# Weight conversion: its addition and subtraction from GpSimd to VectorE, and the norm multiplications of batch 1 from VectorE to GpSimd

## The chip, the cores and the metric

The kernel runs on one core of one Trainium2 chip. The metric is the time of one execution on the device in microseconds (us), the median of several runs. The engines are called as the profile calls them: PE is TensorE (PEld its weight loads), DVE is VectorE, ACT is ScalarE, POOL is GpSimd, SP is SyncE, which here issues the DMAs (SPq is its queue).

## What is computed

The reference takes q, k and v of shape 8 x 12 x 448 x 64 and two weight matrices that the host holds in float64. Eight batches go through attention with a norm, a Fourier mix and a two-layer network:

```python
q_n, k_n = rmsnorm(q, g_q), rmsnorm(k, g_k)       # over the 64 of a head
scores = matmul(q_n, k_n.T) / sqrt(64)
attn = softmax(scores)
x = matmul(attn, v)                               # to (8, 448, 768)
mixed = real(fft(fft(x, axis=1), axis=2))
u = x + mixed
un = (u - mean(u)) / sqrt(var(u) + 1e-6)
out = u + maximum(un @ w_ch1, 0) @ w_ch2          # 768 -> 3072 -> 768
```

## The kernel before

The work is written per batch in two streams. `aux(b)` is the side stream: attention of the six head pairs, then the Fourier mix and the token norm, which leave the input of the network. `ffn(b, unT)` is the main stream: 24 blocks `up(m)` (18 matmuls each, L997) and 36 blocks `down(g, d)` (12 matmuls each, L1018). Batch 0's `aux` stands first; from step 112 on some steps of `aux(1)` go in between. Then `merge` lays `ffn(b)` and `aux(b + 1)` beside each other by a ratio of costs, for batch after batch. The instructions are written in this order; a planner that simulates a timeline when the kernel is built puts each engine's instructions in their final order, and an engine then works through its own queue strictly in that order. An instruction whose input is late holds up all that stand behind it on its engine.

Attention of a pair begins with `norm_pair(b, p)`, numbered `nth = 6 b + p`: ACT squares the raw q and k, DVE sums the squares and scales the sums (tile `ss`), POOL raises them to the power -1/2, and two multiplications of 112 x 512 elements each write the normed q and k (tile `qkn`). The two run on POOL for `nth` 2 to 8, and on DVE for `nth` 0, 1 and from 9 on (L276). Behind them PE transposes `qkn` (tile `qk`). In `softmax_pair` DVE takes the minimum of a score tile in PSUM (`mn`), ACT makes the exponentials (`P`) and their sums (`sm`); batch 0 then has DVE build diagonal matrices (`dg`), with which PE scales, and later batches scale `P` in place, partly on DVE. `fold` is a row of DVE additions and subtractions in SBUF (`eo`, `sd`).

The weights arrive as float64 and are converted to float32 once, in the first batch, and split into a rounded part and a rest; each converted piece goes to DRAM (L807) and is read back from there for later batches. There are 60 pieces: 24 of 128 x 768 elements for the first layer, 36 of 128 x 512 for the second. `convert` (L746) makes one piece of the two 32-bit halves `high` and `low` of each number. In order: ACT takes the absolute value of `high` into `mag` (L756) and scales `low` (L758); DVE clamps, shifts and merges in the sign (L763, L767, L771); POOL adds `low` to `mag` (L775); ACT copies the sum into the rounded part of `w` (L776); POOL subtracts that from the sum, which gives the rest (L777). The helper `behind` only adds ordering edges. The raw halves lie in four `dbl` buffers and the result of the first steps in three `mag` buffers, so that a later piece waits until L777 has freed a `mag` buffer, and its load (L753) until L775 has freed a `dbl` one. Some pieces (`w1e`, `w2e` in names) are converted beside `aux(0)`, the rest when `W1.load` and `W2.load` first reach them. All conversions lie between 20 and 468 us of the trace. The matmuls of `up` and `down` wait for their piece; its DRAM copy and all other loads stand in the one SP queue.

Of the kernel before, what the change touches and what calls it, by code (L numbers as in the profile page):

```python
# [16 lines left out]
ALU = mybir.AluOpType  # L17
# [7 lines left out]
NPAIR = H // 2  # L25
# [66 lines left out]
def spectral_block(ctx, tc, q, k, v, g_q, g_k, w1, w2, d1, d2, out, nb=B):  # L92
    nc = tc.nc
# [27 lines left out]
    V, A, G = Recorded(nc.vector), Recorded(nc.scalar), Recorded(nc.gpsimd)  # L121
    starting = [True]

    def order(ins, before, kind, reason):
        tc.add_manual_dep(
            ins.ins, before.ins.name, mybir.DependencyInfo(kind, reason),
            reason="issue order",
        )
# [3 lines left out]
    def behind(ins):  # L132

        others = given.get(ins.ins.engine, [])
        if ins.ins.engine in gate:
            order(
                ins, gate[ins.ins.engine],
                mybir.DependencyClass.NoSync, mybir.DependencyReason.DATA,
            )
        if starting[0] and len(others) > LAG:  # L140
            order(
                ins, others[-1 - LAG],
                mybir.DependencyClass.NoSync, mybir.DependencyReason.DATA,
            )
# [117 lines left out]
    def norm_pair(b, p):  # L262
        raw = loaded.pop((b, p))
        qk = sb.tile([C, 2, NC, 2, D], F32, tag="qk", name=f"qkn{b}_{p}", bufs=1)
        sq = qk.rearrange("t i c h d -> t (i c h) d")
        flat = raw.rearrange("t i h c d -> t (i h c) d")
        nth = b * NPAIR + p
        A.activation(sq, flat, AF.Square)
        ss = sb.tile([C, 16], F32, tag="ss", name=f"ss{b}_{p}")
        V.tensor_reduce(ss, sq, axis=AX.X, op=ALU.add)  # L270
        V.tensor_scalar(
            out=ss, in0=ss, scalar1=1.0 / D, scalar2=EPS, op0=ALU.mult, op1=ALU.add
        )
        G.tensor_tensor(out=ss, in0=ss, in1=nhalf[:C], op=ALU.pow)
        for i in range(2):
            (G if 2 <= nth < NPAIR * 3 // 2 else V).tensor_tensor(  # L276
                out=qk[:, i].rearrange("t c h d -> t h c d"),
                in0=raw[:, i],
                in1=ss[:, 8 * i : 8 * i + 8]
                .rearrange("t (h c) -> t h c", h=2)[:, :, :, None]  # L280
                .broadcast_to([C, 2, NC, D]),
                op=ALU.mult,
            )
        if plain(b, p):
            return qk, None
        vt = values_of[b, p]
        vhl = sb.tile([128, 4, 4, D], F32R, tag="vhl", name=f"vhl{b}_{p}", bufs=1)
        A.copy(vhl[:, :, ::3], vt)
        (G if b < EARLY else V).tensor_tensor(
            out=vhl[:, :, 1:3], in0=vt, in1=vhl[:, :, ::3], op=ALU.subtract  # L290
        )
        return qk, vhl
# [5 lines left out]
    def plain(b, p):  # L298


        return b * NPAIR + p in PLAIN_PAIRS
# [4 lines left out]
    def transpose_pair(b, p):  # L306
# [3 lines left out]
        load_pair(b, p)  # L310
        load_pair(*next_pair(b, p))
        qk, vhl = norm_pair(b, p)
        yield 0

# [431 lines left out]
    def convert(src, bits, part, name):  # L746

        _, c, f = src.shape  # L750
        raw = sb.tile([128, 1536], U32, tag="dbl", name=f"dbl{name}", bufs=4)
        raw = raw[:, : c * f].rearrange("r (c f w) -> r c f w", c=c, w=2)
        nc.sync.dma_start(raw.rearrange("r c f w -> r c (f w)"), src)  # L753
        low, high = raw[:, :, :, 0], raw[:, :, :, 1]
        value = bits.bitcast(F32)
        first = nc.scalar.activation(value, high.bitcast(F32), AF.Abs)  # L756
        behind(first)
        second = nc.scalar.activation(low, low, AF.Copy, scale=2.0**-29)  # L758
        behind(second)
        order(  # L760
            second, first, mybir.DependencyClass.NoSync, mybir.DependencyReason.DATA
        )
        behind(nc.vector.tensor_scalar(  # L763
            out=value, in0=value, scalar1=MIN_HIGH, scalar2=MAX_HIGH,
            op0=ALU.max, op1=ALU.min,
        ))
        behind(nc.vector.tensor_scalar(  # L767
            out=bits, in0=bits, scalar1=5, scalar2=2,
            op0=ALU.logical_shift_left, op1=ALU.logical_shift_right,
        ))  # L770
        behind(nc.vector.scalar_tensor_tensor(  # L771
            out=bits, in0=high, scalar=0xC0000000, in1=bits,
            op0=ALU.bitwise_and, op1=ALU.bitwise_or,
        ))
        behind(nc.gpsimd.tensor_tensor(out=bits, in0=bits, in1=low, op=ALU.add))  # L775
        behind(nc.scalar.copy(part[0], value))  # L776
        behind(nc.gpsimd.tensor_tensor(  # L777
            out=part[1], in0=value, in1=part[0], op=ALU.subtract
        ))

    class Stream:
# [18 lines left out]
        def converted(self, i, name):  # L800
            hl = self.tile(name)
            src = self.doubles(i)
            bits = sb.tile(
                [128, NR * 128], U32, tag="mag", name=f"mag{self.tag}{name}", bufs=3
            )[:, : self.n * 128].rearrange("r (c f) -> r c f", c=self.n)
            convert(src, bits, [hl[:, k] for k in range(2)], f"{self.tag}{name}")
            nc.sync.dma_start(self.kept(i), hl.bitcast(F32))  # L807
            return hl
# [302 lines left out]
```

## Time and profile before

| | before |
|---|---|
| median of 3 runs | 2161.11 us (2160.51 to 2162.85) |
| span of the profiled execution, first to last instruction | 2158.9 us |
| PE busy | 2088.7 us, 97% |
| DVE busy | 1537.0 us, 71% |
| ACT busy | 1117.9 us, 52% |
| POOL busy | 374.6 us, 17% |

The page gives the span of the profiled execution alone; the median of the timed runs is 2.2 us above it. Busy time is the time in which an engine executes, without its waits for others. A group of the trace names the line of the code, the engine and the operation, the tile written and the tiles read, the shape and the count; then the busy time of the group, the mean duration of one, and the idle time of the engine just before, with what ended it. Most instructions of the attention are recorded through one helper and have the line L115, so they are told apart by their tiles.

### The profile page before, as it was taken

The page shows a single profiled execution, that of the slowest core. Times are in us where ns is not written, and L with a number is a line of the kernel's source. Part 1 is how long each engine was busy: PE and PEld are TensorE (multiplying, and loading weights), DVE is VectorE, ACT ScalarE, POOL GpSimd, SP SyncE. Part 2 cuts the span into 40 slices and gives each one's busy share as a digit, 9 for nine tenths or more (in the row PEclk, how much of TensorE's full clock was granted, in tenths as well). Part 3 has the DMA queues.
Part 4 walks back from the last instruction along what each step waited for, and adds up shares of the span by engine and source line. Part 5 has one row for each costly group of instructions (what it writes and reads, how often), then busy time and mean ns, then how long its engine had stood idle before and what let it go on. Part 6 is the DMA issues. An engine that isn't in the chain of part 4 may idle for free.

```text
span 2158.9 us, 31527 instructions
## 1 busy us (share of the span) xinstructions
PE 2088.7 (97%) x11408; PEld 1838.7 (85%) x11408; DVE 1537.0 (71%) x2809; ACT 1117.9 (52%) x2462; POOL 374.6 (17%) x223
## 2 busy tenths in 40 slices
PE   7978899999999999999999999999999999999998
PEld 4556666789999999999999999999999999998898
DVE  6798889886885778757786678857787578753122
ACT  7877677465652566436653566526563466522100
POOL 4654666340110011001000001100110011000000
PEclk8998999999999999999999999999999999999999
DMA  7555777667555855657555765658555674459664
GB/s 205 178 170 174 249 249 238 224 228 227 161 166 184 250 168 164 195 188 221 175 166 177 231 187 173 194 170 239 179 174 175 204 220 144 150 166 280 217 213 150
DMA packets 294494, 422.12 MB, mean 196 GB/s; under 512 B 182994, under 2 KB 221315, under 8 KB 294340
## 3 DMA queue, kind: packets, MB, share of 16 engines
q1 hardware_dynamic: 293572, 419.43, 62.5%
q8 instruction: 91, 1.49, 0.3%
q10 hardware_dynamic: 768, 0.69, 0.1%
q14 instruction: 63, 0.52, 0.1%
HBM read 360.27 MB, written 65.28 MB: 197 GB/s over the span
## 4 chain that ended last, share of the span: by engine, by line
PE 79%; DVE 2%; DMA 1%; ACT 0%; issue 0%; SPq 0%; ACTq 0%
PE o L1018 29%; PE h L997 29%; PE S L395 5%; PE av L515 4%; PE pt L503 4%; PE y L619 2%; PE qk L340 1%; DMA w<-w 1%; PE oT L935 1%; PE x L651 1%; PE av L520 1%; PE rem L484 1%; PE ab L707 1%; PE un L880 1%; DVE eo L115 0%; DMA ur<-u_dram 0%
## 5 line engine op out<-in xcount | busy, mean ns | idle before, releaser
L1018 PE MATMUL o<-hs,w 128*128 128x448 f32 x3420 | 772.8, 370 | 9.2 <-DMA w<-w 3.0
L997 PE MATMUL h<-unT,w 128*128 128x448 f32 x3402 | 771.1, 371 | 8.4 <-DVE hs L115 6.0
L1018 PEld LDWEIGHTS o<-hs,w 128*128 128x128 f32 x3420 | 632.4, 189 | 63.5 <-issue 6.6
L997 PEld LDWEIGHTS h<-unT,w 128*128 128x128 f32 x3402 | 630.3, 189 | 62.8 <-DVE hs L115 7.0
L115 ACT ACTIVATE P<-S,mn 112x448 f32<-112x448 f32 x384 | 243.5, 636 | 215.2 <-DVE mn L115 202.3
L115 POOL TENSOR_TENSOR ss<-ss,nhalf 112x16 f32<-112x16 f32 x48 | 142.5, 2968 | 912.8 <-DVE ss L115 912.4
L115 DVE TENSOR_REDUCE mn<-S 112x1 f32<-112x448 f32 x384 | 234.5, 618 | 51.1 <-PE S L395 38.9
L115 ACT ACTIVATE hs<-h 128x448 fp32r<-128x448 f32 x192 | 104.1, 542 | 289.7 <-PE h L997 288.2
L115 DVE SCALAR_TENSOR_TENSOR hs<-h,hs 128x448 fp32r<-128x448 f32 x192 | 119.4, 622 | 144.8 <-ACT hs L115 143.5
L115 DVE TENSOR_TENSOR acc<-o,acc 128x448 f32<-128x448 f32 x240 | 148.7, 620 | 87.1 <-PE o L1018 85.8
L115 DVE TENSOR_TENSOR T<-pt,T 128x448 fp32r<-128x448 f32 x216 | 132.5, 620 | 40.2 <-ACT T L115 38.7
L115 ACT CAST T<-pt 128x448 fp32r<-128x448 f32 x216 | 113.3, 531 | 87.3 <-PE pt L503 84.9
L515 PE MATMUL av<-T,vhl 128*128 128x448 f32 x432 | 153.3, 385 | 0.0
L115 DVE TENSOR_SCALAR P<-P,sm 112x448 f32<-112x448 f32 x312 | 136.4, 475 | 5.2
L503 PE MATMUL pt<-ident,P 112*128 112x112 f32 x864 | 120.9, 259 | 0.0
L395 PE MATMUL S<-KD,QT 128*112 128x448 f32 x304 | 117.4, 387 | 3.1 <-ACT KD L115 2.8
L503 PEld LDWEIGHTS pt<-ident,P 112*128 112x128 f32 x864 | 102.6, 140 | 16.6
L395 PE MATMUL S<-rounded,QT 128*112 128x448 f32 x304 | 112.7, 372 | 0.0
L115 POOL TENSOR_TENSOR rstd<-st,nhalf 112x1 f32<-112x1 f32 (+2 forms) x32 | 18.3, 571 | 517.7 <-DVE st L115 517.7
L775 POOL TENSOR_TENSOR magw<-magw,dblw 128x512 uint32<-128x512 uint32 (+1 forms) x45 | 73.9, 1643 | 71.6 <-DVE magw L771 26.3
L515 PEld LDWEIGHTS av<-T,vhl 128*128 128x128 f32 x432 | 80.8, 189 | 6.4
L777 POOL TENSOR_TENSOR w<-magw,w 128x512 fp32r<-128x512 f32 (+1 forms) x45 | 72.3, 1608 | 40.9 <-ACT w L776 27.6
(140 smaller groups left out, 2639.4 us busy)
## 6 DMA issues: line engine op xcount, KB each, us to landing
w<-w SPq DMA_DIRECT2D x285, 512.0 KB, 4.2
w<-w SPq DMA_DIRECT2D x189, 768.0 KB, 5.0
dblw<-w SPq DMA_DIRECT2D x30, 512.0 KB, 5.4
dblw<-w SPq DMA_DIRECT2D x15, 768.0 KB, 5.4
raw<-q SPq DMA_DIRECT2D x96, 112.0 KB, 3.6
raw<-k SPq DMA_DIRECT2D x96, 112.0 KB, 3.9
v<-v SPq DMA_DIRECT2D x96, 96.0 KB, 2.3
u_dram<-u SPq DMA_DIRECT2D x24, 336.0 KB, 3.1
```

The source lines that it names most:

```text
L115: ins = emit(*args, **kwargs)
L340: nc.tensor.transpose(pt[:, c * C : (c + 1) * C], qk[:, i, c].rearrange("t h d -> t (h d)"), ident[:C, :C],)
L395: nc.tensor.matmul(s_, QT[:, h, cs], K[:, h], start=step == 0, stop=step == 1)
L484: nc.tensor.transpose(rem[:, c * C : (c + 1) * C], Pc[c][:, 384:512], ident[:C, :C])
L503: nc.tensor.transpose(pt[:, c * C : (c + 1) * C], Pc[c][:, 512 * h + j * 128 : 512 * h + (j + 1) * 128], ident[:C, :C],)
L515: nc.tensor.matmul(av[:, :S], lv, T[:, i], start=(j == 0 and i == 0), stop=False)
L520: nc.tensor.matmul(av[:, :S], lv, R[:, h], start=False, stop=True)
L619: nc.tensor.matmul(o, src[:, par, t0 : t0 + n], D1[:, ri, par, cols], start=i != 1, stop=i != 0,)
L775: behind(nc.gpsimd.tensor_tensor(out=bits, in0=bits, in1=low, op=ALU.add))
L777: behind(nc.gpsimd.tensor_tensor(out=part[1], in0=value, in1=part[0], op=ALU.subtract))
L997: pace(nc.tensor.matmul(o, w[:, a, c], unT[c][:, z], start=n == 0, stop=n == 17))
L1018: pace(nc.tensor.matmul(o, w[:, a, f], hs[4 * g + f][:, z], start=n == 0, stop=n == 11))
```

## The change

The two POOL instructions of `convert`, the addition L775 and the subtraction L777, become DVE instructions of the same operands. In `norm_pair` the bound up to which POOL does the two multiplications goes from `nth` 9 to `nth` 12, so that the three pairs 9, 10 and 11, the second half of batch 1, have theirs on POOL also. The power stays on POOL; nothing else is touched.

```diff
@@ -273,7 +273,7 @@
         G.tensor_tensor(out=ss, in0=ss, in1=nhalf[:C], op=ALU.pow)
         for i in range(2):
-            (G if 2 <= nth < NPAIR * 3 // 2 else V).tensor_tensor(
+            (G if 2 <= nth < NPAIR * 2 else V).tensor_tensor(
                 out=qk[:, i].rearrange("t c h d -> t h c d"),
@@ -772,9 +772,9 @@
-        behind(nc.gpsimd.tensor_tensor(out=bits, in0=bits, in1=low, op=ALU.add))
+        behind(nc.vector.tensor_tensor(out=bits, in0=bits, in1=low, op=ALU.add))
         behind(nc.scalar.copy(part[0], value))
-        behind(nc.gpsimd.tensor_tensor(
+        behind(nc.vector.tensor_tensor(
             out=part[1], in0=value, in1=part[0], op=ALU.subtract
         ))
```

## Rows read from the trace of the kernel before

**Rows 1.** The page: its span, and the chain that ended last, by engine.
```profile
span 2158.9 us, 31527 instructions
...
PE 79%; DVE 2%; DMA 1%; ACT 0%; issue 0%; SPq 0%; ACTq 0%
```
**Rows 2.** Windows: stretch, its length, busy us (count) of each engine, PE clock, DMA.
```profile
0.00:108.00 108.00, 90.08 (x470) 54.97 (x472) 80.89 (x142) 83.37 (x194) 60.89 (x42) 0.86 0.64 191
108.00:216.00 108.00, 88.39 (x472) 61.75 (x469) 94.70 (x151) 80.50 (x173) 58.21 (x35) 0.86 0.53 172
216.00:486.00 270.00, 247.90 (x1282) 194.50 (x1282) 231.36 (x350) 173.79 (x360) 144.64 (x91) 0.99 0.72 237
486.00:2144.00 1658.00, 1652.86 (x9144) 1519.44 (x9144) 1123.17 (x2155) 780.27 (x1738) 110.87 (x57) 1.00 0.62 191
```
**Rows 3.** Groups of POOL by form, whole span: additions, one of the subtractions, norm multiplications.
```profile
L775 POOL TENSOR_TENSOR magw<-magw,dblw 128x512 uint32<-128x512 uint32 x30 | 43.4, 1448 | 42.7 <-DVE magw L771 12.0 <-issue 12.0 <-DVE sm L115 8.9
L777 POOL TENSOR_TENSOR w<-magw,w 128x512 fp32r<-128x512 f32 x30 | 43.2, 1440 | 23.5 <-ACT w L776 14.0 <-DVE magw L771 2.9 <-DVE magw L763 2.1
L775 POOL TENSOR_TENSOR magw<-magw,dblw 128x768 uint32<-128x768 uint32 x15 | 30.5, 2033 | 28.9 <-DVE magw L771 14.3 <-ACT magw L756 3.9 <-ACT hs L115 2.4
...
L115 POOL TENSOR_TENSOR qkn<-raw,ss 112x512 f32<-112x512 f32 x14 | 18.2, 1319 | 0.3
L775 POOL TENSOR_TENSOR magw1e<-magw1e,dblw1e 128x768 uint32<-128x768 uint32 x9 | 17.1, 1899 | 25.8 <-ACT qkn L115 9.1 <-DVE magw1e L771 6.6 <-ACT w1e L776 3.3
...
L775 POOL TENSOR_TENSOR magw2e<-magw2e,dblw2e 128x512 uint32<-128x512 uint32 x6 | 7.9, 1320 | 22.6 <-ACT qkn L115 11.1 <-DVE magw2e L771 7.7 <-ACT T L115 2.4
```
**Rows 4.** Groups of DVE by form, 0 to 486 us, while conversions run on POOL.
```profile
L115 DVE TENSOR_REDUCE mn<-S 112x1 f32<-112x448 f32 x106 | 63.0, 614 | 12.4 <-PE S L388 6.3 <-ACT P L115 3.1 <-PE S L395 2.7
...
L115 DVE TENSOR_TENSOR qkn<-raw,ss 112x512 f32<-112x512 f32 x16 | 24.3, 1557 | 4.2 <-POOL ss L115 4.2
L767 DVE TENSOR_SCALAR magw<-magw 128x512 uint32<-128x512 uint32 x30 | 21.9, 731 | 0.6
L115 DVE TENSOR_SCALAR P<-P,sm 112x448 f32<-112x448 f32 x32 | 21.8, 691 | 0.6
L115 DVE TENSOR_TENSOR dg<-ident,sm 112x224 f32<-112x224 f32 x24 | 21.7, 910 | 0.4
```
**Rows 5.** The same groups of DVE, 500 to 800 us, after the last conversion.
```profile
L115 DVE TENSOR_REDUCE mn<-S 112x1 f32<-112x448 f32 x60 | 37.0, 619 | 10.0 <-PE S L395 9.4
...
L115 DVE TENSOR_SCALAR P<-P,sm 112x448 f32<-112x448 f32 x60 | 24.5, 450 | 0.9
...
L115 DVE TENSOR_TENSOR qkn<-raw,ss 112x512 f32<-112x512 f32 x14 | 9.1, 685 | 0.1
...
L115 DVE TENSOR_TENSOR vhl<-v,vhl 128x512 fp32r<-128x512 f32 x8 | 5.5, 690 | 4.9 <-ACT vhl L115 4.9
```
**Rows 6.** Single lines and tiles: duration in ns, minimum/median/maximum, first and last start.
```profile
L767 DVE TENSOR_SCALAR magw<-magw x45: 409/560/2126, 187.0 to 448.1; 128x512 uint32<-128x512 uint32 x30, 128x768 uint32<-128x768 uint32 x15
```
```profile
L771 DVE SCALAR_TENSOR_TENSOR magw1e<-dblw1e,magw1e x9: 944/957/1108, 22.8 to 151.8; 128x768 uint32<-128x768 uint32 x9
```
```profile
L115 DVE TENSOR_TENSOR dg<-ident,sm x24: 380/393/2116, 26.2 to 123.3; 112x224 f32<-112x224 f32 x24
```
**Rows 7.** Waits of PE, 0 to 486 us: us in total, times, longest.
```profile
PE S L388 <- ACT P L115: 8.4, 10, 3.2
...
PE un L880 <- DVE unT L115: 0.2, 1, 0.2
```
**Rows 8.** Waits of all engines, 0 to 486 us, those around the conversion.
```profile
ACT P L115 <- DVE mn L115: 37.4, 23, 6.9
...
POOL w L777 <- ACT w L776: 27.6, 10, 9.9
...
ACT magw L756 <- POOL w L777: 21.8, 14, 5.7
...
DVE magw L763 <- ACT magw L756: 14.7, 13, 3.0
```
**Rows 9.** Waits of the SP queue, 0 to 486 us, at the store of a converted piece.
```profile
SPq L807 <- POOL w L777: 70.9, 32, 5.7
```

## The prediction

> **What bounds the kernel now.** I read the page first: the chain that ended last is 79% PE, and no other engine has more than 2% of it [rows 1]. Then the windows, by stage. From 486 us to 2144 us PE is busy for 1652.9 of 1658 us at the full granted clock; nothing that is done for DVE or POOL can shorten that stretch [rows 2]. Before 486 us PE is busy for 90.1 + 88.4 + 247.9 = 426.4 us, so it stands idle for 59.6 us, and in the first 216 us its granted clock averages 0.86. All conversions and all multiplications that the change moves lie in this front. DVE is busy there for 80.9 + 94.7 + 231.4 = 407 us, 84% of the stretch, ACT for 337.7 us, POOL for 263.7 us. So the question is one of 486 us: the change can give back at most a part of the 59.6 us of idle PE, and it loses whatever it makes PE wait longer. The waits of PE in the front, 28 kinds, of which the first and the last stand in [rows 7], add up to 59.9 us: 33.6 us ended by ACT, 22.9 us by DVE, the rest by a DMA and the start. No PE wait is ended by POOL's subtraction or addition: the converted weights themselves are in time.
>
> **Conversion, what comes to DVE.** 60 additions and as many subtractions [rows 3]: the four rows of L775 have the counts 30, 15, 9 and 6, and L777 has the same four. On POOL they take 1320 to 2033 ns each. On DVE the nearest rows are an operation of the same kind and width at 690 ns for 512 columns [rows 5] and a merge of two SBUF operands at 957 ns for 768 columns [rows 6]. With 2 x 36 x 0.690 = 49.7 and 2 x 24 x 0.957 = 45.9 that is +95.6 us of DVE work in the front.
>
> **What leaves DVE again.** DVE pays today for POOL's work, and the trace shows how much. The minimum over scores, which reads PSUM, takes 614 ns beside the conversions and 619 ns after them [rows 4, 5]: nothing. But the operations that work in SBUF are far longer beside them: the scaling of P 691 against 450 ns, the norm multiplication 1557 against 685 ns, the conversion's own shift 731 ns against a shortest of 409 ns, the diagonal matrices 910 on average against a shortest of 380, with single ones of 2116 [rows 4 to 6]. Done for each such group of the front (count times mean less the clean duration; P for instance 32 x 0.241 = 7.7 us, norm 16 x 0.872 = 14.0, diagonals 24 x 0.53 = 12.7), the conversion's own three DVE steps lose 49 us and the others 46 us, together 95 us, an estimate that takes the shortest durations as clean where no later row exists. It is spread over POOL's tensor work: additions 98.9 us and subtractions about as much, norm multiplications 18.2 us [rows 3]. The power, which stays, takes nothing from DVE as far as can be seen: after 486 us POOL has almost only that, and P and norm are at their short durations there [rows 5]. By shares 8% of the 95 us belongs to the norm and stays, some 87 us go.
>
> The Trainium skill (SBUF — State Buffer, Who interferes with whom) says that DVE and GpSimd share one pair of SBUF ports, that it is locked for a whole instruction, and that the loser blocks until the other ends; DVE instructions that read PSUM and SBUF once are free of it. The trace agrees, 614 against 619 ns for the one kind and 1557 against 685 ns for the other. By the rule alone, with every one of the 120 moved POOL instructions holding DVE up to its full 1.3 to 2.0 us, up to 196 us would come free and the sum below would be over 100 us better for DVE; the rows say 87.
>
> **Norm multiplications.** Six instructions of batch 1 leave DVE, 6 x 0.685 = 4.1 us of clean time, and come to POOL, where one is 1319 ns [rows 3]. They bring a little locking with them: 14 of them cost some 8 us now, so six more cost 3.4 us. Cover: POOL has only the power and these left, about 26 us of multiplications in the front instead of 263.7 us busy. If the cover fails, PE's transposes of a pair wait 2 x (1.32 - 0.69) = 1.3 us longer, three times: 4 us at most.
>
> **The balance of DVE** is +95.6 - 87 - 4.1 + 3.4 = about +8 us in 486 us, 2% of its busy time. So the change is, for DVE, an exchange of blocked time for work of its own. Cost at the end: between nothing (DVE has 79 us idle in the front) and 8 us. I take 0.5 us, by PE's 22.9 us of direct waits for 407 us of DVE work.
>
> **Releases from POOL.** ACT begins a piece when a `mag` buffer is free and stands 21.8 us for that behind POOL's subtraction [rows 8], and some 4 us at its copy for the addition; exponentials and copies for PE are queued behind it. ACT's idle time in the front is 486 - 337.7 = 148 us; POOL's 25.8 us are 17% of it, and 17% of PE's 33.6 us for ACT is 5.9 us. Bounds: a gain of 0 (the wait for POOL becomes a wait for DVE) to 21.8 us. I take 5.9. The store in the SP queue waits 70.9 us for the subtraction [rows 9], with the loads of q, k, v and weights behind it; hardly any PE wait is ended by a DMA, so its gain is taken as nothing.
>
> **Long pieces in DVE's queue.** Blocked instructions of 1.5 to 2.1 us [rows 4, 6] stand in front of those for which PE and ACT wait: the longest wait of ACT for a minimum is 6.9 us [rows 8]. DVE-rooted waits of PE are 22.9 us plus the part of the 33.6 us that ACT itself passes on from DVE (65.7 of its 148 us, 44%): 15 us. Together 38 us, of which the blocked share of DVE's time, 95 of 407 us or 23%, is 8.7 us. The added instructions stand in the same queue, but none is longer than 0.96 us. I take half, 4.4 us of gain; bounds 5 us of loss and 8.7 us of gain.
>
> **The new wait.** The subtraction needs ACT's copy of the sum (L776), and now DVE, not POOL, stands in front of it; behind it are minima, rests of `hs` and `acc`, for which PE and ACT wait. POOL waits for that copy 27.6 us in 10 times, the longest 9.9 us [rows 8]. How long DVE would wait no row shows. Nearest is DVE's clamp, which waits in the same way for ACT's first step: 14.7 us for 45 pieces [rows 8], 0.33 us each, and over the 60 that is 17 to 20 us; the bounds are 0, if the planner puts other work between, and 28 us as on POOL. I take 17 us of DVE time, which at the rate of 38 us of PE wait for 407 us of DVE work is 1.6 us; if DVE becomes the bound it is all 17.
>
> **The clock.** At 0.86 over 178.5 us of busy PE, 25 us of work at full speed are lost [rows 2]. With about 10 of 59.6 us of idle time gone, the same share of 25 is 4 us; I take half, 2 us.
>
> **Sum**: +0.5 - 5.9 - 4.4 + 1.6 - 2 = -10.2 us. The span 2158.9 becomes 2148.7, and with the 2.2 us that the median lies above it, 2151 us.
>
> **Rivals.** First, no change that can be told from the measurement (0.2% is 4.3 us, about what a measurement of this kernel can resolve): waits for POOL become waits for DVE of the same length, and only the balance and the clock remain, 2160 us. For it: DVE's load is nearly the same. Against it: two engines' queues then share what three did, and an exact balance needs luck.
>
> Second, slower: DVE becomes the bound of the front. Its 407 us become 415, the copies add 17, which is 432, and its present idle time less the wait for the clamp, 79 - 17 = 62 us, is mostly waiting for ACT and PE and may stay. That is 494 us for what must fit into 486, and with the copy at POOL's 28 us it is 505: +8 to +19 us, say 2171 us. It decides from about 0.3 us of wait for each copy on, if the other waits don't shrink. For it: DVE is already at 84%, and in 108 to 216 us at 88% [rows 2]. Against it: the waits in its idle time are in part those for ACT, which POOL holds up now.
>
> Third, the change doesn't free DVE: POOL's remaining instructions block it as much, since the multiplications lie beside more of its SBUF work, and the 95.6 us come on top. DVE would need 500 us without any wait: 2190 us or more. Against it speak the clean durations after 486 us, where the power runs on POOL [rows 5].
>
> **How the numbers follow.** Forecast (faster, about 2151, its own range 2134 to 2157) 0.50; no change 0.22; DVE the bound 0.25; not freed 0.03. The predicted time is 2151 us. Downward, ACT's 21.8 us and 8.7 us at their bounds with no new wait would give 2128 us; that end isn't likely in full, and I take 2134. Upward I take 2170, near the middle of the second rival. Faster by over 0.2%: 0.50; within: 0.22; slower: 0.28.
>
> **What would show it.** Between 0 and 486 us the mean of P falls to about 450 ns and the diagonals to about 390; additions and subtractions on DVE are near 690 and 957 ns; DVE's busy time stays within some 15 us of 407; ACT's 21.8 us for POOL are gone; DVE's wait at L777 for ACT's copy is near 17 us; PE's idle time before its full stretch falls from 59.6 to some 50 us. A DVE wait at L777 above 30 us, or P still near 690 ns, would make the prediction wrong. So would a PE busy share below 0.88 between 216 and 486 us.

## The result, and the profile after

The changed kernel takes 2136.89 us (median of 4 runs, 2135.72 to 2138.99) against 2161.59 us for the kernel before in the same comparison: a ratio of 0.988, with an interval of 0.9869 to 0.9891. That is 24.7 us less. The forecast was 2151 us, about 10 us less: the direction was right and the time lies inside the range, but the gain is more than twice what was forecast, so the working has a wrong size in it.

The page of the changed kernel has a span of 2136.9 us and PE 98% busy. The windows below have the same stretches as [rows 2], up to the end of PE's full stretch; the columns are the stretch, its length, the busy time and count of PE, PEld, DVE, ACT and POOL, the granted clock and the DMA.

```profile
0.00:108.00 108.00, 87.60 (x462) 50.84 (x463) 83.48 (x158) 83.61 (x194) 31.68 (x23) 0.89 0.65 191
108.00:216.00 108.00, 90.94 (x491) 63.32 (x490) 94.35 (x177) 82.55 (x179) 25.83 (x16) 0.86 0.50 162
216.00:486.00 270.00, 267.81 (x1409) 216.43 (x1408) 236.47 (x452) 185.22 (x384) 28.33 (x13) 0.99 0.83 268
486.00:2122.00 1636.00, 1631.66 (x9003) 1497.60 (x9002) 1107.59 (x2123) 770.32 (x1710) 111.33 (x57) 1.00 0.62 189
```

In the first 216 us PE is busy for 178.5 us, exactly as before: nothing was gained there. Between 216 and 486 us PE is busy for 267.8 us in place of 247.9: 19.9 of the 22.0 us by which the two profiled spans differ. DVE's busy time there is 236.5 us, not less than the 231.4 of before, though more work was done in the time. So the stretch has to be cut by work, not by the clock. From here on "the first network stage" is the stretch from the first matmul of batch 0's `up` (L997) to some 0.6 us before the end of the last of its `down` (L1018), in all runs alike. First the kernel before, then the changed one, the same columns:

```profile
181.80:476.00 294.20, 269.73 (x1381) 210.86 (x1382) 255.11 (x374) 198.27 (x405) 162.51 (x99) 0.98 0.70 232
```
```profile
184.10:448.30 264.20, 262.00 (x1367) 207.19 (x1366) 237.81 (x446) 193.64 (x390) 32.20 (x15) 0.99 0.78 256
```

The stage is 30.0 us shorter, and PE's idle time in it falls from 24.5 to 2.2 us. The other 7.7 us are busy time of PE: it does 14 matmuls fewer in the stage (1367 for 1381), side work that comes later, and its granted clock averages 0.99 in place of 0.98. The stage starts 2.3 us later than before and side work follows it, so the end gains less than the stage.

The groups of DVE between 0 and 486 us in the changed kernel, which answer to [rows 4], and the moved steps:

```profile
L115 DVE TENSOR_REDUCE mn<-S 112x1 f32<-112x448 f32 x112 | 68.0, 620 | 14.2 <-PE S L388 10.4 <-PE S L395 3.6
L777 DVE TENSOR_TENSOR w<-magw,w 128x512 fp32r<-128x512 f32 x30 | 21.2, 707 | 0.9 <-ACT w L776 0.8
L775 DVE CUSTOM_DVE_ANT_0 magw<-dblw,magw 128x1024 uint16<-128x1024 uint16 x30 | 21.0, 700 | 0.0
L115 DVE TENSOR_SCALAR P<-P,sm 112x448 f32<-112x448 f32 x38 | 16.8, 457 | 0.3
...
L767 DVE TENSOR_SCALAR magw<-magw 128x512 uint32<-128x512 uint32 x30 | 12.9, 434 | 0.1
L115 DVE TENSOR_TENSOR dg<-ident,sm 112x224 f32<-112x224 f32 x24 | 11.5, 492 | 0.2
...
L115 DVE TENSOR_TENSOR qkn<-raw,ss 112x512 f32<-112x512 f32 x10 | 6.6, 688 | 3.8 <-POOL ss L115 3.7
```

P falls from 691 to 457 ns, the shift from 731 to 434, the diagonals from 910 to 492, the norm multiplication from 1557 to 688, while the minimum, which reads PSUM, stays at 620. And the waits of ACT inside the stage (182 to 476 us before, 184 to 448 us after); a line has the total, the times and the longest:

```profile
ACT P L115 <- DVE mn L115: 26.7, 15, 6.9
ACT magw L756 <- POOL w L777: 21.8, 14, 5.7
```
```profile
ACT hs L115 <- PE h L997: 18.3, 9, 4.0
...
ACT magw L756 <- DVE w L777: 7.5, 8, 1.8
ACT P L115 <- DVE mn L115: 7.3, 7, 2.9
```

Before, ACT waits most for DVE's minima and for POOL; after, it waits most for PE, which is idle for only 2.2 us. The stage has become PE's.

### The profile page after: what moved, and what is told of

The parts are those of the page before. It is cut to its first block, busy times and chain, and to the rows that moved or that the text cites. A ratio compares the mean times of both kernels' runs of the same rounds, so it can differ in the third digit from the quotient of the medians.

```text
span 2136.9 us, 31453 instructions
## 1 busy us (share of the span) xinstructions
PE 2087.4 (98%) x11408; PEld 1836.2 (86%) x11408; DVE 1528.7 (72%) x2923; ACT 1121.7 (52%) x2462; POOL 197.2 (9%) x109
## 4 chain that ended last, share of the span: by engine, by line
PE 91%; DVE 3%; DMA 2%; ACT 2%; SPq 1%; issue 1%; POOL 1%; POOLq 0%; ACTq 0%; DVEq 0%
PE h L997 32%; PE o L1018 32%; PE S L395 5%; PE av L515 4%; PE pt L503 4%; PE y L619 2%; PE qk L340 1%; PE S L388 1%; PE av L455 1%; DMA w<-w 1%; PE x L651 1%; PE oT L935 1%; PE pt L442 1%; PE rem L484 1%; PE ab L707 1%
## 5 line engine op out<-in xcount | busy, mean ns | idle before, releaser
L1018 PE MATMUL o<-hs,w 128*128 128x448 f32 x3420 | 775.5, 371 | 2.6 <-DMA w<-w 2.6
L997 PE MATMUL h<-unT,w 128*128 128x448 f32 x3402 | 767.4, 370 | 0.4 <-ACT unT L115 0.3
L1018 PEld LDWEIGHTS o<-hs,w 128*128 128x128 f32 x3420 | 633.9, 189 | 58.4 <-issue 6.5
L997 PEld LDWEIGHTS h<-unT,w 128*128 128x128 f32 x3402 | 628.5, 188 | 54.7 <-issue 4.1
L115 DVE TENSOR_SCALAR P<-P,sm 112x448 f32<-112x448 f32 x312 | 128.9, 451 | 4.8
L503 PEld LDWEIGHTS pt<-ident,P 112*128 112x128 f32 x864 | 102.8, 140 | 16.4
L115 ACT ACTIVATION_READ_ACCUMULATOR P<-S,mn 112x1 f32 x384 | 75.8, 197 | 0.0
L115 DVE TENSOR_REDUCE ss<-qkn 112x16 f32<-112x1024 f32 x48 | 58.4, 1216 | 16.9 <-ACT qkn L115 16.6
```

What stands on the lines that cost most here:

```text
L115: ins = emit(*args, **kwargs)
L503: nc.tensor.transpose(pt[:, c * C : (c + 1) * C], Pc[c][:, 512 * h + j * 128 : 512 * h + (j + 1) * 128], ident[:C, :C],)
L997: pace(nc.tensor.matmul(o, w[:, a, c], unT[c][:, z], start=n == 0, stop=n == 17))
L1018: pace(nc.tensor.matmul(o, w[:, a, f], hs[4 * g + f][:, z], start=n == 0, stop=n == 11))
```

## The experiments

Four theories were set against each other. **Ports**: POOL's tensor work blocked DVE's SBUF instructions. **Chain**: every piece passed POOL twice, and ACT, DVE and the `mag` buffers waited for that. **Norm**: the multiplications of pairs 9 to 11 leaving DVE. **Plan**: the planner's other order of instructions, which no run tests by itself, since every version is planned anew. The table collects all runs. Ratios are to the kernel before in the same comparison, with their 95% interval; the other columns are of the profiled run: where the first network stage starts, its length, and PE's idle and DVE's busy time in it, in us, as in the two windows above.

| run | median us | ratio to before | start | length | PE idle | DVE busy |
|---|---|---|---|---|---|---|
| before | 2161 to 2164 | 1 | 181.8 | 294.2 | 24.5 | 255.1 |
| changed | 2136.89 | 0.988 (0.9869 to 0.9891) | 184.1 | 264.2 | 2.2 | 237.8 |
| e1_conv_only | 2136.88 | 0.9875 (0.986 to 0.9889) | 182.9 | 265.3 | 6.0 | 238.2 |
| e2_norm_only | 2161.32 | 0.9986 (0.9976 to 0.9996) | 183.4 | 292.2 | 21.9 | 253.2 |
| e3_mag4 | 2159.82 | 0.9982 (0.9972 to 0.9991) | 180.8 | 290.1 | 16.4 | 251.1 |
| e4_pool_load | 2179.02 | 1.0071 (1.0056 to 1.0086) | 190.4 | 296.5 | 27.1 | 283.6 |
| e5_early_dve | 2164.44 | 1.0009 (0.9999 to 1.0018) | 183.0 | 291.2 | 21.1 | 251.4 |
| e6_late_dve | 2133.69 | 0.9868 (0.9853 to 0.9882) | 182.3 | 260.7 | 2.3 | 236.9 |
| e7_add_dve | 2146.00 | 0.9926 (0.9911 to 0.9941) | 185.1 | 270.2 | 9.9 | 242.2 |
| e8_sub_dve | 2148.22 | 0.9939 (0.9922 to 0.9955) | 179.6 | 278.5 | 16.1 | 244.7 |
| e9_pool_pow | 2127.51 | 0.9833 (0.9819 to 0.9848) | 175.2 | 262.1 | 3.1 | 236.6 |
| e10_sub_twice | 2156.84 | 0.9968 (0.9957 to 0.998) | 182.7 | 287.2 | 16.4 | 274.1 |
| e11_late_ahead | 2151.69 | 0.9944 (0.9926 to 0.9961) | 199.2 | 261.6 | 2.6 | 237.2 |
| e12_chain | 2186.41 | 1.0114 (1.0097 to 1.0131) | 177.7 | 322.5 | 35.6 | 258.7 |
| e13_chain_short | 2153.76 | 0.995 (0.9932 to 0.9968) | 186.9 | 277.9 | 11.8 | 242.7 |
| e14_chain_first | 2130.37 | 0.9838 (0.9818 to 0.9859) | 178.9 | 261.3 | 3.7 | 236.9 |
| e15_chain_second | 2135.14 | 0.9867 (0.9851 to 0.9883) | 178.9 | 269.0 | 7.4 | 242.9 |

### The two parts of the change, each alone

e1 takes the conversion's two lines from the change and leaves the norm as before; e2 takes the norm line alone:

```diff
-            (G if 2 <= nth < NPAIR * 3 // 2 else V).tensor_tensor(   # e2 alone
+            (G if 2 <= nth < NPAIR * 2 else V).tensor_tensor(
-        behind(nc.gpsimd.tensor_tensor(out=bits, in0=bits, in1=low, op=ALU.add))   # e1 alone
+        behind(nc.vector.tensor_tensor(out=bits, in0=bits, in1=low, op=ALU.add))
```

> Only the conversion's addition and subtraction go to DVE; the norm multiplications of pairs 9 to 11 stay on DVE as before. Theory 1 (ports: POOL's tensor work blocked DVE's SBUF work in the first network stage, from about 200 to 460 us): nearly the whole gain, 2137 to 2143 us, P near 450 ns, and the six norm multiplications near 690 ns each instead of 679 to 4325. Theory 2 (chain: each piece waited for POOL's slow steps and ACT for the mag buffer): the same time. Theory 3 (norm: the gain comes from taking the multiplications of pairs 9 to 11, 14.6 us of DVE time, off DVE): 2155 us or more.

> Only the norm multiplications of pairs 9 to 11 go to POOL; the conversion stays on POOL. Theory 1 (ports): no gain to speak of, 2156 to 2168 us, with P still near 690 ns. Theory 2 (chain): slower by some us, since POOL's queue gets 6 x 1.3 us more ahead of additions and subtractions, 2162 to 2170 us. Theory 3 (norm): 2140 to 2150 us.

The conversion alone gives the whole gain, 2136.88 us. The norm alone gives 0.14%, some 3 us. Its trace says the same: with the norm moved, DVE is busy for 253.2 us in the stage, a little less than before, and the stage is 292.2 us long, 2.0 us less. The norm theory falls.

### Which half of the pieces

In e5 only the pieces converted before the network stage have their addition and subtraction on DVE, in e6 only those from its start on:

```diff
+        behind((nc.vector if starting[0] else nc.gpsimd).tensor_tensor(   # e5; e6 the other way round
```

> The kernel before; only the pieces converted while batch 0's attention and Fourier mix run (before the first network stage, up to about 190 us) have addition and subtraction on DVE. Norm as before. By the trace of the changed kernel, whose PE progress at 190 us is the same as before's, this gains nothing: 2157 to 2165 us. If freed DVE time counted the same everywhere, it would have a third of the gain, 2152 us.

> The other half: only the pieces converted from the start of the first network stage on (from about 190 us) have addition and subtraction on DVE. If the gain lies in that stage alone: 2137 to 2145 us, with PE idle under 6 us between 216 and 486 us. If it is spread over both: about 2148 us.

The early half gains nothing, the late half all and a little more (2133.69 us, below both expectations). Before the stage PE waits, before and after, for chains through DVE and ACT of batch 0's attention (before: 35.2 us of idle PE up to 181.8 us; changed: 37.5 us up to 184.1 us). Freed DVE time does not reach PE there.

### Tensor work on POOL that nobody needs

The changed kernel, with 120 additions on POOL of a tile of its own, each released by a step of the conversion:

```diff
+        for after in (added, copied):
+            idle = nc.gpsimd.tensor_tensor(out=held, in0=held, in1=held, op=ALU.add)
+            order(idle, after, Sync, SCHED_ONLY)
```

> The changed kernel, and after each addition and after each ACT copy of a piece POOL adds a 128x512 tile of its own to itself, 120 times, about 1.3 us each; nothing waits for the result but POOL's own queue (the power and the norm). Theory 1 (ports): DVE's SBUF work is blocked again, P back above 600 ns, DVE's busy time before 486 us up by 50 us or more on top of the 95.6 us that it took over, and PE is held up: 2165 to 2200 us. Theory 2 (chain) and theory 4 (the planner's other order of instructions, not the ports): the conversion's chain doesn't pass POOL, so 2136 to 2145 us.

2179.02 us, 42 us above the changed kernel. First POOL's group, then two DVE groups of 0 to 486 us:

```profile
L785 POOL TENSOR_TENSOR held<-held 128x512 f32<-128x512 f32 x120 | 174.8, 1457 | 182.1 <-ACT w L779 70.0 <-DVE magw L777 39.6 <-DVE magw2e L777 26.7
```
```profile
L769 DVE TENSOR_SCALAR magw<-magw 128x512 uint32<-128x512 uint32 x30 | 19.0, 633 | 0.2
L115 DVE TENSOR_SCALAR P<-P,sm 112x448 f32<-112x448 f32 x26 | 16.9, 653 | 0.1
```

P is back from 457 to 653 ns, the shift from 434 to 633. In the stage DVE is busy 45.8 us longer than in the changed kernel, with as many instructions (446), and the stage is 32.3 us longer: 0.71 us for each us of blocked DVE. It also starts 6.3 us later, so not all of the 42 us lie in it.

To see whether it was POOL's queue rather than the blocking, e9 keeps POOL as busy with powers, which are long but touch few elements:

```diff
-                out=held, in0=held, in1=held, op=ALU.add,      # 128x512, twice a piece
+                out=held, in0=held, in1=nhalf, op=ALU.pow,     # 128x16, once a piece
```

> The changed kernel, and after each ACT copy of a piece POOL raises a tile of its own of 128x16 elements to a power, 60 times, about 3 us each (180 us of POOL, as much as the 120 additions of the load on POOL took). Theory 1 (ports): the power takes nothing from DVE, P stays near 455 ns, 2136 to 2143 us. Rival: the load on POOL was slow because the power and the norm multiplications of the pairs stood behind it in POOL's queue; then this is as slow, 2170 us or more.

```profile
L785 POOL TENSOR_TENSOR held<-held,nhalf 128x16 f32<-128x16 f32 x60 | 201.1, 3351 | 90.2 <-ACT w L779 64.6 <-ACT w1e L779 14.0 <-ACT w2e L779 9.9
```
```profile
L115 DVE TENSOR_SCALAR P<-P,sm 112x448 f32<-112x448 f32 x40 | 17.5, 454 | 0.3
L769 DVE TENSOR_SCALAR magw<-magw 128x512 uint32<-128x512 uint32 x30 | 13.4, 451 | 0.2
```

POOL is busier than with the additions, 201.1 us against 174.8, and P (454 ns), the shift and the stage (262.1 us) are those of the changed kernel. So the blocking of DVE, not POOL's queue, made e4 slow. The time, 2127.51 us, is even 9 us below the changed kernel and below both expectations; the stage is as long, but it starts at 175.2 us in place of 184.1. Why the stretch ahead of it is shorter here was not tried. Over all runs that start lies between 175 and 199 us; the stage's length, with all late pieces on DVE, no added tensor work on POOL or DVE and at most one added power for each piece on the way, between 261 and 269. In the kernel before, e2, e3 and e5, where the late pieces have both steps on POOL, it is between 290 and 294. So the stage tells causes apart better than the median does, and the planner's order, new in each of these runs, moves its length by less than the conversion does.

### A microsecond of DVE work instead of blocking

e10 makes the subtraction twice:

```diff
+        for _ in range(2):
             behind(nc.vector.tensor_tensor(
                 out=part[1], in0=value, in1=part[0], op=ALU.subtract
```

> The changed kernel with the subtraction made twice on DVE: 36 x 0.69 + 24 x 0.957 = 47.8 us more of DVE work, which nothing blocks and which the planner knows of. If a microsecond of DVE costs the end as much whether it is work or blocked time (the load on POOL cost 42 us for some 63 us of blocked DVE time, 0.67 each), +32 us, about 2169 us. If blocked time is dear because it makes single instructions long where the planned order doesn't allow for it, and planned work is cheap: up to +10 us, 2137 to 2147 us.

2156.84 us, 20 us above the changed kernel and between the two expectations. DVE is busy 36.2 us longer in the stage, and the stage is 23.0 us longer, 0.63 us for each. That is nearly the price of blocked time in e4. The idea that blocked time is dear and planned work cheap falls: added to the 237.8 us of DVE in the changed kernel's stage, a microsecond of either makes the stage 0.63 to 0.71 us longer.

If that price also holds between 237.8 and the 255.1 us of the kernel before, the 17.3 us that DVE's busy time fell give 11 to 12 of the 30 us, an estimate. Some 18 remain.

### One step alone, and the mag buffers

> The kernel before with the addition alone on DVE; the subtraction stays on POOL. Theory 1 (ports): half of the blocking goes, 2145 to 2154 us. Theory 2 (chain): the piece still ends with POOL's subtraction, which frees the mag buffer, so ACT's wait of 21.8 us stays for the most part and little is gained, 2154 to 2162 us.

> The kernel before with the subtraction alone on DVE; the addition stays on POOL. Theory 1 (ports): half of the blocking goes, 2145 to 2154 us, like the addition alone. Theory 2 (chain): DVE frees the mag buffer but ACT's copy waits for POOL's addition and DVE for the copy, so DVE waits at its subtraction, and the gain is under 6 us, 2155 us or more.

> The kernel before with four mag buffers in place of three, nothing else. Theory 2 (chain): ACT's 21.8 us of waiting for POOL's subtraction fall below 8 us and PE's idle time in the first network stage falls with it, 2142 to 2152 us. Theory 1 (ports): the blocked time of DVE stays, P near 690 ns, and the time stays within 2157 to 2165 us.

Each of the two steps alone on DVE (one of the change's two lines each) gives more than half of the gain: 2146.00 and 2148.22 us. That agrees with the ports theory, and contradicts the chain theory in the form in which it was put, that the one step left on POOL keeps the cost. But DVE's busy time is not all of it here either: it falls by 12.9 and 10.4 us against the kernel before, and the stage by 24.0 and 15.7, of which 0.63 to 0.71 for each us explains 8 to 9 and 7. And the addition left alone on POOL (e8) is not free: its stage is 14.3 us longer than the changed kernel's, with 6.9 us more DVE.

A fourth `mag` buffer (`bufs=4` in place of 3, nothing else) gave 0.18% and a stage of 290.1 us, and P and the shift stayed as slow as before, 725 and 795 ns. But the wait that it was to shorten became longer, 30.5 us in place of 21.8:

```profile
ACT magw L756 <- POOL w L777: 30.5, 15, 5.5
```

So this run does not show what that wait costs.

### The chain through POOL, without its tensor work

e12 leads each piece through POOL twice again, with small powers that leave DVE alone: 128x8 after the addition, for which ACT's copy waits, and again after the subtraction, reading `mag`. e13 does the same with one column, e14 has only the first step, e15 only the second.

```diff
+        slow = through_pool(added)        # POOL: ones ** value[:, 0, :8]; not in e15
         copied = nc.scalar.copy(part[0], value)
+        order(copied, slow, Sync, SCHED_ONLY)
         rest = nc.vector.tensor_tensor(out=part[1], in0=value, in1=part[0], op=ALU.subtract)
+        through_pool(rest)                # not in e14; e13: value[:, 0, :1]
```

> The changed kernel with the conversion's chain led through POOL again but without POOL's tensor work: after the addition POOL raises 128x8 ones to powers that it reads from the mag buffer (some 1.7 us by the 3 us that 16 columns take), ACT's copy waits for that, and after the subtraction POOL does the same again, so that it also holds the mag buffer. DVE's own work is that of the changed kernel. Theory 2 (chain: the waits of ACT and DVE for POOL's slow steps and for the mag buffer cost the first network stage some 18 of its 30 us): that stage grows from 264 us by 10 to 18 us, 2147 to 2157 us. Theory 1 (ports alone: what cost the time was that POOL's tensor work made DVE's SBUF instructions long): the stage stays at 260 to 268 us, 2127 to 2141 us, P near 455 ns.

> As the chain run, but POOL raises one column instead of eight, 0.55 us in place of 1.69 us, so that a piece passes POOL twice for a third of the time; nothing else differs. If the cost of the chain goes with the time that a piece spends on POOL, a third of its 49 us: about 2153 us, with ACT waiting some 22 us for POOL at its first step, which is what it waited before the change. If it is the two more handovers as such, nearly as slow as the chain run, 2175 us or more. If a wait of that size is free, 2137 to 2143 us; then ports alone explain the change.

> As the chain run, with POOL's first step alone: 1.69 us between the addition and ACT's copy, the place of the addition on POOL; the mag buffer is freed by DVE's subtraction or by POOL's step, whichever is later. If the latency ahead of the copy matters, DVE and PE wait for the piece: 2150 to 2165 us. If the hold of the mag buffer matters, 2137 to 2146 us.

> As the chain run, with POOL's last step alone: after DVE's subtraction POOL reads the mag buffer for 1.69 us more, so that ACT begins a later piece later. If the hold of the mag buffer matters: 2150 to 2175 us, with ACT waiting 30 us or more for POOL at its first step; if only the latency ahead of the copy does, 2137 to 2146 us.

With both steps the time is 2186.41 us, worse than before the change and far above both expectations, though P is at 453 ns. With both steps shorter (0.86 us on average against 1.88) it is 2153.76 us. With either step alone the time is not above the changed kernel's and below all that was expected of it: 2130.37 and 2135.14 us. But both stages start 5.2 us earlier than there; in length, e14's is 2.9 us shorter, e15's 4.8 us longer, with 5.2 us more idle PE. Waits of ACT up to 500 us, in e12, e13, e14 and e15:

```profile
ACT magw L758 <- POOL ones L780: 66.8, 32, 6.4
```
```profile
ACT magw L758 <- POOL ones L780: 23.9, 15, 5.4
...
ACT w L791 <- POOL ones L780: 8.2, 10, 1.5
```
```profile
ACT magw L758 <- DVE w L797: 19.8, 14, 3.4
...
ACT w L791 <- POOL ones L780: 7.0, 8, 1.5
```
```profile
ACT magw L758 <- POOL ones L780: 20.2, 14, 4.6
```

ACT's wait for the buffer is about the same in e13, e14 and e15, 20 to 24 us, so the size of that wait does not tell the cost; that was the expectation's mistake. What e12 and e13 have and e14 and e15 don't is that the two steps of different pieces share POOL's one queue. The wait of POOL for the subtraction, in e12 and in e13:

```profile
POOL ones L780 <- DVE w L797: 86.0, 34, 8.6
```
```profile
POOL ones L780 <- DVE w L797: 123.9, 34, 19.8
```

While POOL stands there, the first step of the next piece stands behind it. The kernel before had the same shape: an addition and a subtraction of each piece in one queue, with the subtraction waiting 27.6 us for ACT's copy [rows 8]. That this sharing is the cause is not shown, though. In e15, with one step, POOL waits 98.2 us for the subtraction, more than in e12, and ACT's copy waits for the first step about as long in e13 (8.2 us) as in e14 (7.0). In e12 the pieces themselves come late: PE waits 12.2 us for ACT's copy of them, a wait that the kernel before does not have; and 33.4 of the 58.3 us by which the stage is longer are idle PE, while the rest is PE being busy longer, at a granted clock of 0.94 against 0.99. In e13, 7.0 of the 11.8 us of idle PE are one single wait. Lines of e13's timeline in order (start and duration in us; in brackets the idle time before and what ended it), and PE's behind them:

```profile
367.73 0.95 DVE L797 TENSOR_TENSOR w<-magw,w 128x768 fp32r<-128x768 f32 x1
...
368.83 3.27 POOL L780 TENSOR_TENSOR ones<-ones,magw 128x1 f32<-128x1 f32 x1 [3.16 <-DVE w L797]
...
370.61 1.10 DVE L115 TENSOR_TENSOR tot<-eo,eo 128x900 f32<-128x900 f32 x1
...
372.13 0.66 ACT L758 ACTIVATE magw<-dblw 128x512 f32<-128x512 f32 x1 [5.37 <-POOL ones L780]
```
```profile
374.25 0.74 PE L1040 MATMUL o<-hs,w 128*128 128x448 f32 x1 [6.98 <-ACT T L115]
```

From 367.73 to 371.71 us DVE works in SBUF without a break. The power of one column, whose shortest takes 0.54 us, starts in the middle of that, takes 3.27 us and ends at 372.10; ACT's first step of a later piece has waited 5.37 us for the `mag` buffer that it frees, and the copies behind it in ACT's queue, for which PE waits, come late by that. So a wait of ACT for a `mag` buffer can reach PE through ACT's queue, as the forecast's term for the releases assumed.

## Why the prediction was wrong in size

**The bound** was read rightly as the front, but by the clock and not by stages. The 59.6 us of idle PE in 486 us were treated as one pool. In fact 35.2 us lie before the network stage, where nothing came back, and 24.5 us in it, where nearly all came back. PE's idle time up to 486 us fell to 39.7 us, not to some 50.

**What comes to DVE**: 95.6 us were forecast. The moved steps measure 98.1 us in the eight groups of L775 and L777; two of them stand above, and four are

```profile
L775 DVE CUSTOM_DVE_ANT_0 magw<-dblw,magw 128x1536 uint16<-128x1536 uint16 x15 | 15.2, 1016 | 0.0
L777 DVE TENSOR_TENSOR w<-magw,w 128x768 fp32r<-128x768 f32 x15 | 14.3, 952 | 0.4 <-ACT w L776 0.2
...
L775 DVE CUSTOM_DVE_ANT_0 magw1e<-dblw1e,magw1e 128x1536 uint16<-128x1536 uint16 x9 | 8.6, 957 | 0.1
L777 DVE TENSOR_TENSOR w1e<-magw1e,w1e 128x768 fp32r<-128x768 f32 x9 | 8.6, 954 | 0.1
```

**What leaves DVE**: 87 us were forecast. DVE's busy time over the whole span went from 1537.0 to 1528.7 us; with 98.1 us more and 4.1 us of norm less, 102 us must have gone. So the balance of DVE is -8 us, not +8. Of the signs of clean DVE time that were named, P at 450 and steps at 690 and 957 ns nearly came, and so did a busy time near 407 us (414.3); the diagonals at 390 ns did not: they measure 492, with POOL's norm multiplications still beside them.

**Balance, long pieces**: +0.5 and -4.4 us, so 3.9 us of gain. This is the step that failed: the price of a microsecond of DVE. The measured counterpart is 11 to 12 us of stage, 17.3 us less DVE at the 0.63 to 0.71 that e10 and e4 gave. The rate used, PE's waits per us of DVE work over the front (38 of 407, or 0.09), was an average over a stretch where freed DVE time gave nothing (e5) and one where added DVE time costs 0.63 to 0.71.

**Releases from POOL**: -5.9 us, a share of ACT's idle time. Whether this term was too small as well stays open, since no run prices it as it stood. Some 18 of the 30 us of stage remain for it and for all else that DVE's busy time does not cover, the clock among it. ACT waits for POOL at its first step 21.8 us in the kernel before, 20.2 in e15 and 23.9 in e13; the stages of these two are 4.8 and 13.7 us longer than the changed kernel's, and 5 us more DVE time in each explains about 3 of that. That leaves some 1 to 10 us for such a wait, an estimate from these two stages; so the 18 us are what is left over and not a measured price of the releases.

**The new wait**: +1.6 us, from 17 us of DVE waiting at the subtraction. The trace shows 3.2 us (2.2 and 1.0 in two groups). So the wait was put at five times its size; the rival that hung on it, DVE waiting in front of L777, did not come. But its bound is real: e10, with 36 us more DVE time in the stage, lost most of the gain.

**The norm**: up to 4 us either way were named, 3 us of gain were measured alone and none together with the rest (e1 against the changed kernel).

**The clock**: -2 us, looked for in the first 216 us. There it rose a little, 0.89 and 0.86 against 0.86 and 0.86, without a gain in PE's busy time. In the stage it is 0.99 against 0.98: before, it averages 0.97 from 250 to 300 and from 300 to 350 us, after, only from 350 to 400 us. One hundredth of that stage is about 3 us, an estimate: the size is near the forecast, the place is not.

**The rivals.** Unfreed DVE was excluded by P at 457 ns. No change took the waits for DVE to be as long as those for POOL: ACT's 21.8 us became 7.5. DVE as the bound took DVE's other idle time to stay and 17 us of new waits to come: 3.2 came.

**Open**: how the 30 us of stage divide between ports, the chain through POOL, the clock and the plan. 12 and 18 rest on one price from e4 and e10, which have more DVE work than either kernel, and on stages whose side work differs a little: the changed one has 72 DVE instructions more, not the 84 that the change brings into it. And why the start of the stage moves by several us between plans (e9, e11, e14), which is as large as many effects looked for here. Of e11, the late half on DVE with the side steps beginning four steps earlier, 2125 to 2138 us were expected and 2151.69 measured; it is only known that the stage began at 199.2 us.

The late half alone (e6), with 2133.69 us, and e9 and e14, with 2127.51 and 2130.37 us, are below both kernels. In e9 and e14 it is mostly the earlier start of the stage (8.9 and 5.2 us), less its length (2.1 and 2.9 us).

## What to carry to other kernels

Cut a front into stages before sharing out idle time: freed DVE time was worth nothing ahead of the network stage (e5), while each microsecond added in it cost 0.63 to 0.71. Price moved work by what the helper engine blocks as well as by what it does, reading the same group's duration with and without the helper beside it. And look at what stands behind a wait in an in-order queue: ACT's wait for a buffer held up the copies that PE needed. One short power on a piece's way cost little here, two cost 14 and 58 us of stage; whether it was the number of passes is not shown.

## What was unexpected of the hardware

Not every POOL instruction holds DVE up. The additions of 128x512 (1457 ns each) made P 653 ns; 201.1 us of powers of 128x16 (3351 ns each) left it at 454. The Trainium skill (SBUF — State Buffer, Who interferes with whom) says that whoever issues first has the shared ports for its whole instruction and the other blocks fully. For the additions the runs agree. For the powers they don't: by that rule sixty instructions of 3.4 us would have blocked DVE often. But in the first 486 us of e9 each DVE instruction that took over 0.25 us more than the shortest of its group overlapped a norm multiplication of POOL's; beside powers alone the excess is at most 0.2 us. The measurement decides. In the kernel before there are single exceptions, such as a `dg` of 1990 ns at 73.09 us with POOL in a power.

It also goes the other way: the powers are long when DVE works in SBUF. The same power took 2.9 to 5.6 us in e9 and 0.54 to 3.27 us in e13. In e13 DVE is in instructions whose tiles all lie in SBUF for 82% of the time of the 32 powers above 0.94 us, and for 27% of that of the 57 below 0.6 us. The durations (minimum, median, maximum in ns):

```profile
L785 POOL TENSOR_TENSOR held<-held,nhalf x60: 2892/3249/5599, 33.2 to 431.0; 128x16 f32<-128x16 f32 x60
```
```profile
L780 POOL TENSOR_TENSOR ones<-ones,magw x90: 536/696/3273, 196.6 to 462.9; 128x1 f32<-128x1 f32 x90
```

An addition of 32-bit integers that took POOL 1448 ns for 512 columns runs on DVE in 700 ns; the trace records it as one custom operation over 1024 16-bit values.
